# q in units of 512 tokens of two heads from the second batch, the last 64 tokens of all heads as one unit, k and v loaded by pairs of heads

## The chip, the cores and the metric

One core of one Trainium2 chip runs one program. The metric is the device time of an execution in microseconds (us); of several runs the median is given.

## The reference

Two layers, one behind the other. The first is a linear attention with feature maps, for 8 batches of 8 heads, 576 tokens and 64 dimensions; the second a feed-forward network (FFN) with an exact GELU on the 4608 tokens of 512 numbers that the heads give side by side.

```python
def phi(x):                                   # w_phi: 64 x 128
    proj = np.einsum('bhsd,df->bhsf', x, w_phi)
    proj = proj - np.max(np.abs(proj), axis=-1, keepdims=True)
    return np.concatenate([np.exp(proj), np.exp(-proj)], axis=-1)
q_p, k_p = (phi(q), phi(k))
kv = np.einsum('bhsf,bhsd->bhfd', k_p, v)
z = np.sum(k_p, axis=2)
num = np.einsum('bhsf,bhfd->bhsd', q_p, kv)
den = np.einsum('bhsf,bhf->bhs', q_p, z)[..., None] + 1e-06
x = (num / den).transpose(0, 2, 1, 3).reshape(4608, 512)
h = x @ w_in                                  # 512 x 2048
out = (0.5 * h * (1.0 + erf(h / sqrt(2)))) @ w_out   # 2048 x 512
```

## The kernel before

**How the order is made.** The program isn't written in the order in which it runs. Every operation is put into a plan (class `Plan`) with its engine, an estimated cost, a rank, the buffers it reads and writes, and the number of places that each buffer has. `order()` (L109) plays the engines through: at each step the engine that can start first takes its operation with the lowest rank. On TensorE (PE) attention products have a rank lower by `PULL`, but are held back while FFN products run until they sum up to `LUMP` us or one of them has waited for `LINGER` us (L183), so that they come in lumps between FFN products. `emit()` (L245) writes the operations in the order of their planned starts. On the chip each engine, and SP, which issues nearly all DMAs, goes through its own list in that order and waits where an operand isn't there yet. The constants at L790 to L824 are the planner's.

**Attention**, batch after batch (`attention`, L560). `k_rest` and two times `k_quad` (L452) make the sums over k: a quad is two pairs of heads. Per quad one load brings k into kt (524 KB), one v into vt (665 KB); each has two places. Per pair, `k_unit` projects k on PE (pk, eight products of 128 columns), DVE takes the maximum of the magnitudes (mx) and subtracts it, ACT takes both exponentials (ek), PE sums them with v (kv, 40 products of 65 columns, the last of which gives z), and ACT copies that to kvn. The last 64 tokens of k of all heads go through one smaller unit first (pk_r, er).

`q_pair` (L484) then takes the 576 tokens of a pair of heads in two halves of 288 (`HS`): a load (qt), the projection of both heads on PE (pq, the "q unit", two products), a copy by ACT into pc, the maximum over partitions by GpSimd (POOL: `partition_all_reduce`, mb), a subtraction on DVE, two exponentials on ACT (ef). In batches 0 and 1 (`ND`) the product with kvn gives numerator and denominator together (the "d unit", 65 rows). From batch 2 on the numerators are a product of their own ("n unit", pn), and the denominators go another way: DVE weighs the features with z (un), POOL sums them over partitions (db), and row 0 is stored to d_d. xo carries the numerators to x_d in DRAM. `quotients` (L549) loads the denominators of one half of a batch (dc), takes the reciprocal and stores it to r_d.

**FFN.** 18 blocks of 256 tokens. `tokens` (L581) loads a block's numerators (xr, from x_d) and reciprocals (into xh, from r_d), and DVE multiplies and splits the product into a high and a low part (xh, xl). In blocks 0 to 7 (`block`, L623) `up` makes twelve products of 256 columns into ph for each 128 hidden units, ACT takes the GELU twice, DVE the low part (gl), and PE the down-projection into po. The 32 pieces of w_in and w_out are loaded and split by DVE and ACT at the start (`split_weight`), into places named w_i and w_o. Blocks 8 to 17 (`seven`, L695) need a down-projection of seven block products in place of eight; for it sums of w_out's quarters are made (planned from 177.8 us on) and stored to t_d, and `fetch_sums` (L682) loads them into tw0 to tw7. These places lie where attention's lay, so their loads wait for the last operation that uses a place of `EARLIER` (L300).

Places that the change touches: `EARLIER = dict(kr=1, kt=2, vt=2, mx=2, er=2, ek=2, kvn=4, un=1, db=1, qt=2, pc=2, mb=1, ef=2, xo=2, dc=2)`. Products of attention are in plain fp32, and each leaves two records in the trace (an n unit eight, a k projection sixteen); FFN's are in a shorter type and leave one. All matrix products go through the helper at L330, so rows name them by their tiles; likewise the subtractions and additions of L371 and the copies of L365.

Of the kernel before, what the change touches and what calls it, by code (L numbers as in the profile page):

```python
# [59 lines left out]
class Plan:  # L60
# [227 lines left out]
def fused_kernel(ctx: ExitStack, tc: tile.TileContext, qT, kT, va, w_st, w_in, w_out, out):  # L288
# [131 lines left out]

    def k_unit(b, nm, kt, at, cs, e, early, k):
# [26 lines left out]

    def k_quad(b, g, kvs, rank, rest):  # L452
# [9 lines left out]
        for p in range(2):  # L462
            e = [sb[EARLY_EK[p] if b == 0 else "ek"]([P, 2, 4, NF], F32, f"ek_{nm}_{p}_{s}") for s in (1, 0)][::-1]
            k_unit(b, f"{nm}_{p}", kt, lambda c: kt()[:, c * P : (c + 1) * P], range(4 * p, 4 * p + 4), e, EARLY_PK[p] if b == 0 else "pp", k)
            acc = ps["kv"]([P, 4, D + 1], F32, f"kv_{nm}_{p}")
# [15 lines left out]
            kvs[2 * g + p] = kvn  # L481


    def q_pair(b, p, kvs, rank, halves=(0, 1)):  # L484
# [4 lines left out]
        for half in halves:  # L489
            nm = f"{b}_{p}_{half}"  # L490
            ss = slice(half * HS, half * HS + HS)
            qt = sb["qt"]([P, HS], F32, f"qt_{nm}")
# [4 lines left out]
            op("pe", PAIR_Q, lambda pq=pq, qt=qt: [
                mm(pq()[:, j, :HS], lhsT=wst()[64 * j : 64 * j + 64], rhs=qt()[64 * j : 64 * j + 64], start=True, stop=True) for j in range(2)
            ], r=[qt, wst], w=[pq], also=[pc], kind="q", **k(1))
            copy("act", act(2 * HS, True), pc, lambda pq=pq: pq()[:, :, :HS], [pq], [pc], **k(1))  # L500
            op("pool", 2.28, lambda mb=mb, pc=pc: nc.gpsimd.partition_all_reduce(  # L501
                mb(), pc(), P, bass_isa.ReduceOp.absmax), r=[pc], w=[mb], port="max", **k(1))
            tt("dve", dve(2 * HS), pc, pc, mb, ALU.subtract, [pc, mb], [pc], **k(1))
# [362 lines left out]
```

## Time and profile before

| | before |
|---|---|
| median of 3 runs | 1075.69 us (1075.23 to 1076.4) |
| profiled execution | 1074.26 us, span 1072.5 us |
| granted clock of PE, mean | 0.986 |
| PE busy | 1040.8 us (97%) |
| weight loads on PE (beside the products) | 910.0 us (85%) |
| DVE busy | 737.5 us (69%) |
| ACT busy | 617.5 us (58%) |
| POOL busy | 328.2 us (31%) |
| DMA | 107.11 MB, mean 100 GB/s |

The span goes from the first to the last instruction of the profiled execution; its own time is 1.8 us longer. Busy times count instructions in work, whichever engine they wait for otherwise. PE is the engine to follow: a share of 97% says that little of the span passes without a product, but not which of the products' time is columns and which is the step from one kind of product to another; that takes pieces of the chain of waits from single stretches. A granted clock of 1.00 is the higher of PE's two levels (2.4 GHz).

### The profile page before, as it was taken

How to read it: one execution, taken by the hardware profiler on the slowest of the kernel's cores; microseconds unless marked ns; L12 is line 12 of the kernel's file. 1: busy time of each engine (PE TensorE's matmuls, PEld its weight loads, DVE VectorE, ACT ScalarE, POOL GpSimd, SP SyncE). 2: the span in 40 equal slices, each digit the busy share in tenths (PEclk: the TensorE clock that was granted, in tenths of full speed). 3: DMA queues.
4: the chain of work that ended last, by engine and by line, in shares of the span. 5: the costliest groups of instructions: out<-in, count | busy, mean ns of one | idle time of the engine just before them, and what ended most of it. 6: DMA issues, size and time to landing. Idle time of an engine off the chain costs nothing.

```text
span 1072.5 us, 24197 instructions
## 1 busy us (share of the span) xinstructions
PE 1040.8 (97%) x9855; PEld 910.0 (85%) x9855; DVE 737.5 (69%) x1327; ACT 617.5 (58%) x1067; POOL 328.2 (31%) x116
## 2 busy tenths in 40 slices
PE   7979989999999999999999999999999999999997
PEld 4647857887887888787788889999999999999997
DVE  4989999979988999757657532566466465565454
ACT  4867878676866776677676633344344344343343
POOL 2231033645566665866766520000000000000000
PEclk7988999999999999999999999999999999999999
DMA  7676564335344434322122158021021021021000
GB/s 266 214 205 194 176 192 123 102 113 166 103 134 141 134 110 143 94 80 83 46 59 71 37 182 296 21 61 41 20 60 41 21 60 40 20 61 40 2 21 20
DMA packets 87393, 107.11 MB, mean 100 GB/s; under 512 B 25121, under 2 KB 68289, under 8 KB 87281
## 3 DMA queue, kind: packets, MB, share of 16 engines
q1 hardware_dynamic: 87136, 105.30, 32.3%
q8 instruction: 77, 1.26, 0.5%
q14 instruction: 36, 0.29, 0.1%
q10 hardware_dynamic: 144, 0.26, 0.1%
HBM read 75.87 MB, written 29.66 MB: 98 GB/s over the span
## 4 chain that ended last, share of the span: by engine, by line
PE 78%; DVE 11%; ACT 5%; issue 3%; DMA 2%; POOL 0%; SPq 0%; ACTq 0%; POOLq 0%; DVEq 0%
PE ph L330 33%; PE po L330 13%; PE pa L330 10%; PE pb L330 8%; PE pn L330 5%; PE kv L330 4%; PE pq L330 3%; PE pk L330 2%; DVE pc L371 1%; ACT ek L440 1%; DVE ts L371 1%; DVE mx L435 1%; DMA xh<-r_d 1%; DVE ek L371 1%; ACT L632 1%
## 5 line engine op out<-in xcount | busy, mean ns | idle before, releaser
L330 PE MATMUL ph<-xh,w_i 128*128 128x256 f32 x2304 | 413.3, 277 | 0.0
L330 PEld LDWEIGHTS ph<-xh,w_i 128*128 128x128 f32 x2304 | 355.9, 188 | 4.7 <-issue 4.2
L330 PE MATMUL ph<-xl,w_i 128*128 128x256 f32 x1152 | 318.6, 277 | 0.0
L536 POOL PARTITION_ALL_REDUCE db<-un x48 | 183.9, 3831 | 128.6 <-DVE un L533 123.1
L330 PEld LDWEIGHTS ph<-xl,w_i 128*128 128x128 f32 x1152 | 216.3, 188 | 0.4
L501 POOL PARTITION_ALL_REDUCE mb<-pc x64 | 147.1, 2299 | 169.9 <-ACT pc L365 116.0
L371 DVE TENSOR_TENSOR sg<-ga 128x256 f32<-128x256 f32 (+1 forms) x240 | 84.7, 376 | 149.7 <-ACT ga L709 149.0
L330 PE MATMUL po<-w_o,gh 128*128 128x512 f32 (+1 forms) x519 | 164.8, 399 | 2.4 <-DVE w_o L371 1.9
L709 ACT ACTIVATE ga<-ph 128x512 f32<-128x512 f32 x80 | 48.0, 600 | 158.3 <-PE ph L330 156.6
L330 PEld LDWEIGHTS po<-w_o,gh 128*128 128x128 f32 x519 | 93.3, 188 | 30.7 <-issue 4.7
L330 PE MATMUL pa<-w_o,oh 128*128 128x256 f32 x640 | 112.8, 276 | 0.0
L330 PE MATMUL pn<-ef,kvn 128*64 128x288 f32 (+1 forms) x512 | 97.4, 423 | 8.9 <-ACT xo L365 8.9
L507 ACT ACTIVATE ef<-pc 128x576 f32<-128x576 f32 x128 | 82.2, 678 | 39.5 <-DVE pc L371 31.4
L330 PE MATMUL po<-w_o,gl 128*128 128x512 f32 (+1 forms) x288 | 101.0, 369 | 0.3 <-DVE gl L371 0.3
L330 PEld LDWEIGHTS pa<-w_o,oh 128*128 128x128 f32 x640 | 96.2, 188 | 0.0
L371 DVE TENSOR_TENSOR gl<-ph,gh 128x512 fp32r<-128x512 f32 x64 | 43.9, 687 | 64.7 <-ACT ph L633 60.6
L330 PE MATMUL pa<-w_o,ol 128*128 128x256 f32 x320 | 88.3, 276 | 0.0
L371 DVE TENSOR_TENSOR pc<-pc,mb 128x576 f32<-128x576 f32 x64 | 77.7, 1215 | 14.4 <-POOL mb L501 14.3
L440 ACT ACTIVATE ek<-ek 128x1024 f32<-128x1024 f32 x64 | 67.9, 1061 | 31.4 <-DVE ek L371 30.6
L330 PE MATMUL pb<-tw,uh 128*128 128x256 f32 x480 | 85.6, 276 | 0.0
L330 PEld LDWEIGHTS pn<-ef,kvn 128*64 128x64 f32 (+1 forms) x512 | 39.7, 138 | 41.3 <-ACT xo L365 15.8
L330 PEld LDWEIGHTS pb<-tw,uh 128*128 128x128 f32 x480 | 72.2, 188 | 0.0
(71 smaller groups left out, 1610.4 us busy)
## 6 DMA issues: line engine op xcount, KB each, us to landing
vt<-in_va_dram SPq DMA_DIRECT2D x16, 650.0 KB
t_d<-ts SPq DMA_DIRECT2D x40, 256.0 KB
qt<-in_qT_dram SPq DMA_DIRECT2D x64, 144.0 KB
out_dram<-ob SPq DMA_DIRECT2D x35, 256.0 KB
kt<-in_kT_dram SPq DMA_DIRECT2D x16, 512.0 KB
raw_i<-in_w_in_dram SPq DMA_DIRECT2D x16, 512.0 KB
raw_o<-in_w_out_dram SPq DMA_DIRECT2D x16, 512.0 KB
x_d<-xo SPq DMA_DIRECT2D x48, 144.0 KB
```

Of the source, the lines that this page charges most:

```text
L330: return tc.keep_in_program_order(nc.tensor.matmul(*a, **kw))
L371: op(eng, cost, lambda: e.tensor_tensor(out=dst(), in0=a(), in1=b(), op=o), r=r, w=w, **kw)
L435: op("dve", dve(256 * n, True), lambda: nc.vector.tensor_reduce(out=mx(), in_=xs(), axis=AX.X, op=ALU.max, apply_absolute_value=True), r=[ ...
L440: op("act", act(256 * n), lambda s=s: nc.scalar.activation(e[s](), e[1](), AF.Exp, scale=1.0 - 2.0 * s), r=[e[1]], w=[e[s]], table="exp", ...
L501: op("pool", 2.28, lambda mb=mb, pc=pc: nc.gpsimd.partition_all_reduce(mb(), pc(), P, bass_isa.ReduceOp.absmax), r=[pc], w=[mb], port="max ...
L507: op("act", act(2 * HS), lambda ef=ef, pc=pc, s=s: nc.scalar.activation(ef()[:, s], pc(), AF.Exp, scale=1.0 - 2.0 * s), r=[pc], w=[ef], ta ...
L536: op("pool", 3.8, lambda db=db, un=un: nc.gpsimd.partition_all_reduce(db(), un(), P, bass_isa.ReduceOp.add), r=[un], w=[db], port="add", * ...
L632: op("act", act(2 * TB, True) + 0.016, lambda gh=gh, ph=ph: nc.scalar.activation(gh(), ph(), AF.Gelu), r=[ph], w=[gh], table="gelu", rank= ...
L709: op("act", act(2 * TB, True) + 0.037, lambda ph=ph, ga=ga: nc.scalar.activation(ga(), ph(), AF.Gelu), r=[ph_all], w=[ga], table="gelu", a ...
```

## The change

From batch 1 on the 576 tokens of a pair of heads are cut into 512 and 64 where they were cut into 288 and 288 (`PIECES`); batch 0 stays at 288. The first 512 tokens go through `q_pair` as one unit of twice 512 columns. The last 64 tokens of all four pairs go through a new function, `q_rest`, as one unit of twice 256 columns: one projection, one maximum, one subtraction and two exponentials for all eight heads; the numerators (16 small products, since each head has its own kvn for either sign) fill one PSUM tile, and are stored to x_rest, which `tokens` loads with one DMA. `q_front` and `q_sum` hold what both have in common. The sum of the weighed features is written over pc, so un has no places of its own any more. The two exponentials have a tile each (ef, three places). kvn has seven places in place of four, and zb keeps z of all pairs for the rest unit. The quotients of the 512 tokens are taken before the rest unit, those of the 64 behind it.

k and v are loaded by pairs of heads: kt 262 KB, vt 333 KB, eight loads a batch for four. From batch 1 on kt and vt have one place each, of a pair's size; batch 0's eight loads have places of their own, those of w_o8 to w_o15, which are free until these weights come. The projection of k waits for the rest unit's projection two batches before (`behind`), an order among PE's own instructions. The planner's costs are extended by the new POOL shapes, and fourteen of its constants have new values; two of them stand below.

```diff
+HM = 512
+HR = S - HM
+PIECES = [((0, HS), (HS, HS))] + [((0, HM), (HM, HR))] * (B - 1)
...
-    EARLIER = dict(kr=1, kt=2, vt=2, mx=2, er=2, ek=2, kvn=4, un=1, db=1, qt=2, pc=2, mb=1, ef=2, xo=2, dc=2)
+    EARLIER = dict(kr=1, kt=1, vt=1, mx=2, er=2, ek=2, kvn=7, zb=2, db=1, qt=2, pc=2, mb=1, ef=3, xo=2, dc=2)
...
-        op("pe", n * PAIR_K, proj, r=[kt, wst], w=[x], also=[mx], kind="k", **k())
+        op("pe", n * PAIR_K, proj, r=[kt, wst], w=[x], also=[mx], kind="k", behind=last_pq.get(b - 2, ()), **k())
...
+    early = lambda i: plan.pool(spool, f"w_o{8 + i}", 1)
...
-        kt = sb["kt"]([P, 8 * P], F32, f"kt_{nm}")
-        op("sp", 0.06, lambda: nc.sync.dma_start(out=kt(), in_=kT[b, g, :, : 8 * P]), w=[kt], kb=524, **k())
-        vt = sb["vt"]([P, 20, D + 1], F32, f"vt_{nm}")
-        op("sp", 0.06, lambda: nc.sync.dma_start(out=vt(), in_=va[b, g]), w=[vt], kb=665, **k())
+        kts, vts = [], []
         for p in range(2):
+            kt = (early(4 * g + p) if b == 0 else sb["kt"])([P, 4 * P], F32, f"kt_{nm}_{p}")
+            op("sp", 0.06, lambda kt=kt, p=p: nc.sync.dma_start(out=kt(), in_=kT[b, g, :, 4 * P * p : 4 * P * (p + 1)]), w=[kt], kb=262, **k())
+            vt = (early(4 * g + 2 + p) if b == 0 else sb["vt"])([P, 10, D + 1], F32, f"vt_{nm}_{p}")
+            op("sp", 0.06, lambda vt=vt, p=p: nc.sync.dma_start(out=vt(), in_=va[b, g, :, p]), w=[vt], kb=333, **k())
...
+            if b >= ND:
+                if "z" not in kvs:
+                    kvs["z"] = sb["zb"]([P, 4, 4], F32, f"zb_{b}")
+                z = kvs["z"]
+                op("act", act(4) + 0.05, lambda z=z, kvn=kvn, p=p: nc.scalar.copy(out=z()[:, 2 * g + p], in_=kvn()[:, :, D]), r=[kvn], w=[z], **k())
...
+    def q_front(nm, n, load, kb, k, main):
+        qt = sb["qt"]([P, n], F32, f"qt_{nm}")
+        op("sp", 0.06, lambda: load(qt), w=[qt], kb=kb, **k(1))
+        pc = sb["pc"]([P, 2, n], F32, f"pc_{nm}")
+        mb = sb["mb"]([P, 2, n], F32, f"mb_{nm}")
+        pq = ps["pp"]([P, 2, 512], F32, f"pq_{nm}")
+        pq_op = op("pe", n * 4 / 2400 + 0.014, lambda: [
+            mm(pq()[:, j, :n], lhsT=wst()[64 * j : 64 * j + 64], rhs=qt()[64 * j : 64 * j + 64], start=True, stop=True) for j in range(2)
+        ], r=[qt, wst], w=[pq], also=[pc], kind="q", **k(1))
+        copy("act", act(2 * n, True), pc, lambda: pq()[:, :, :n], [pq], [pc], **k(1))
+        most = f"max{main}"
+        op("pool", plan.SPENT[most], lambda: nc.gpsimd.partition_all_reduce(
+            mb(), pc(), P, bass_isa.ReduceOp.absmax), r=[pc], w=[mb], port=most, **k(1))
+        tt("dve", dve(2 * n), pc, pc, mb, ALU.subtract, [pc, mb], [pc], **k(1))
+        ef = [sb["ef"]([P, 2, n], F32, f"ef_{nm}_{s}") for s in range(2)]
+        for s in range(2):
+            op("act", act(2 * n), lambda s=s: nc.scalar.activation(ef[s](), pc(), AF.Exp, scale=1.0 - 2.0 * s), r=[pc], w=[ef[s]], table="exp", **k())
+        return pc, ef, pq_op
+
+    def q_sum(nm, n, pc, k, main):
+        db = sb["db"]([P, 2, n], F32, f"db_{nm}")
+        total = f"add{main}"
+        op("pool", plan.SPENT[total], lambda: nc.gpsimd.partition_all_reduce(db(), pc()[:, :2], P, bass_isa.ReduceOp.add), r=[pc], w=[db], port=total, **k())
+        return db
...
-            ss = slice(half * HS, half * HS + HS)
-            qt = sb["qt"]([P, HS], F32, f"qt_{nm}")
...
-            mb = sb["mb"]([P, 2, HS], F32, f"mb_{nm}")
...
-            op("pe", PAIR_Q, lambda pq=pq, qt=qt: [
...
-            ef = sb["ef"]([P, 2, 2, HS], F32, f"ef_{nm}")
+            at, n = PIECES[b][half]
+            main = "" if n == HS else " main"
+            pc, ef, _ = q_front(nm, n, lambda qt, at=at, n=n: nc.sync.dma_start(out=qt(), in_=qT[b, p, :, at : at + n]), n * 0.512, k, main)
...
-            un = sb["un"]([P, 2, HS], F32, f"un_{nm}")
-            db = sb["db"]([P, 2, HS], F32, f"db_{nm}")
...
+            one = lambda s, j, kvn=kvn: kvn()[:, 2 * s + j, D : D + 1]
+            for j in range(2):
+                op("dve", dve(n, fast=True) + 0.06, lambda pc=pc, ef=ef, one=one, j=j: nc.vector.tensor_scalar(
+                    out=pc()[:, j], in0=ef[0]()[:, j], scalar1=one(0, j), scalar2=None, op0=ALU.mult), r=[ef[0], kvn], w=[pc], **k())
+            for j in range(2):
+                op("dve", dve(n) + 0.06, lambda pc=pc, ef=ef, one=one, j=j: nc.vector.scalar_tensor_tensor(
+                    out=pc()[:, j], in0=ef[1]()[:, j], scalar=one(1, j), in1=pc()[:, j], op0=ALU.mult, op1=ALU.add),
+                   r=[ef[1], kvn, pc], w=[pc], **k())
+            db = q_sum(nm, n, pc, k, main)
...
+            pn = ps["pn"]([P, n], F32, f"pn_{nm}")
+            op("pe", n * 8 / 2400 + 0.012, lambda pn=pn, kvn=kvn, ef=ef: [
+                mm(pn()[64 * j : 64 * j + 64], lhsT=kvn()[:, 2 * s + j, :D], rhs=ef[s]()[:, j], start=s == 0, stop=s == 1)
                 for s in range(2) for j in range(2)
...
+    def q_rest(b, kvs, rank):
+        k = lambda x=0: dict(rank=next(rank))
+        plan.stream = "q"
+        nm, n = f"{b}_rest", 4 * HR
+        pc, ef, pq_op = q_front(nm, n, lambda qt: nc.sync.dma_start(
+            out=qt().rearrange("r (p t) -> r p t", p=4), in_=qT[b, :, :, HM:].rearrange("p r t -> r p t")), 131, k, " rest")
+        last_pq[b] = [pq_op]
+        kv = [kvs[p] for p in range(4)]
+        of = lambda s, j, p: ef[s]()[:, j, p * HR : (p + 1) * HR]
...
+        if b < ND:
+            for j in range(2):
+                pn = ps["pn"]([P, n], F32, f"pn_{nm}_{j}")
+                op("pe", 8 * mm4_cost(D + 1, HR), lambda pn=pn, j=j: [
+                    mm(pn()[: D + 1, p * HR : (p + 1) * HR], lhsT=kv[p]()[:, 2 * s + j, :], rhs=of(s, j, p), start=p == 0 and s == 0, stop=p == 3 and s == 1,
+                       skip_group_check=True) for p in range(4) for s in range(2)], r=[*kv, *ef], w=[pn], kind="d", **k())
...
+            return
+        z = kvs["z"]
+        un = sb["pc"]([P, 4, n], F32, f"un_{nm}")
+        for s in range(2):
+            tt("dve", dve(2 * n), lambda s=s: un()[:, 2 * s : 2 * s + 2].rearrange("r j (p t) -> r j p t", p=4),
+               lambda s=s: ef[s]().rearrange("r j (p t) -> r j p t", p=4),
+               lambda s=s: z()[:, :, 2 * s : 2 * s + 2].rearrange("r p j -> r j p").unsqueeze(3).to_broadcast([P, 2, 4, HR]), ALU.mult, [ef[s], z], [un], **k())
+        tt("dve", dve(2 * n), lambda: un()[:, :2], lambda: un()[:, :2], lambda: un()[:, 2:], ALU.add, [un], [un], **k())
+        db = q_sum(nm, n, un, k, " rest")
+        for j in range(2):
+            op("sp", 0.06, lambda j=j: nc.sync.dma_start(out=heads(j), in_=db()[:1, j].rearrange("o (p t) -> o p t", p=4)), r=[db], w=[d_d[b][1]], kb=1, **k())
+        pn = ps["pn"]([P, n], F32, f"pn_{nm}")
+        op("pe", 8 * PAIR_V, lambda: [
+            mm(pn()[64 * j : 64 * j + 64, p * HR : (p + 1) * HR], lhsT=kv[p]()[:, 2 * s + j, :D], rhs=of(s, j, p), start=p == 0 and s == 0, stop=p == 3 and s == 1,
+               skip_group_check=True) for p in range(4) for s in range(2) for j in range(2)], r=[*kv, *ef], w=[pn], kind="n", **k())
...
-                q_pair(b, p, kvs, rank)
-        for half in range(2):
-            quotients(b, half, rank)
+                q_pair(b, p, kvs, rank, (0,))
+        quotients(b, 0, rank)
+        q_rest(b, kvs, rank)
+        quotients(b, 1, rank)
...
+            kw = dict(w=[xr], rank=rank(0) - 8)
+            if b and h:
+                op("sp", 0.06, lambda b=b, s=s, n=n, o=o: nc.sync.dma_start(out=xr()[:, :, o : o + n], in_=x_rest[b]()[:, :, s : s + n]),
+                   r=[x_rest[b]], kb=n * 2.048, **kw)
...
-LUMP = 5.47
-LINGER = 4.41
+LUMP = 5.52
+LINGER = 3.07
```

In the built program, PE's list around the numerators of batch 5's first pair, before (ph: up-projection of block 4; pn: numerators; pq: projection of q; the number behind a name only tells tiles apart):

```order
L330 MATMUL ph_4_2_5125<-xl_4_3975,w_i3_1_1073 128x256
L330 MATMUL ph_4_2_5125<-xh_4_3786,w_i3_1_1073 128x256
L330 MATMUL pn_5_0_0_5166<-ef_5_0_0_5079,kvn_5_0_0_4467 64x288 x4
L330 MATMUL pq_5_1_0_5175<-qt_5_1_0_4908,wst_114 128x288 x2
L330 MATMUL ph_4_3_5180<-xh_4_3786,w_i0_1_862 128x256
L330 MATMUL ph_4_3_5180<-xl_4_3975,w_i0_1_862 128x256
```

and after (po: down-projection of block 4; kv: sums over k of batch 6):

```order
L334 MATMUL po_4_4862<-w_o3_786,gh_4_1_4860 128x512 x2
L334 MATMUL po_4_4862<-w_o3_786,gl_4_1_4874 128x512
L334 MATMUL pn_5_0_0_4914<-ef_5_0_0_0_4871,kvn_5_0_0_4137 64x512 x2
L334 MATMUL pn_5_0_0_4914<-ef_5_0_0_1_4893,kvn_5_0_0_4137 64x512 x2
L334 MATMUL kv_6_0_0_4924<-vt_6_0_0_4669,er_6_0_4717 64x65 x2
L334 MATMUL kv_6_0_0_4924<-vt_6_0_0_4669,er_6_1_4709 64x65 x2
```

The n unit of 288 columns with the q unit of the next pair behind it has become one n unit of 512 columns, and a kv unit of batch 6 stands behind it.

SP's list at the start of the program, behind the load of w_phi, before (kr, kt and vt: k and v of batch 0; raw: the first piece of w_in):

```order
L447 DMA kr_0_120<-in_kT_dram 128x2x128
L459 DMA kt_0_0_122<-in_kT_dram 128x1024
L461 DMA vt_0_0_124<-in_va_dram 128x1300
L459 DMA kt_0_1_126<-in_kT_dram 128x1024
L461 DMA vt_0_1_128<-in_va_dram 128x1300
L383 DMA raw_i0_0_131<-in_w_in_dram 128x512
```

and after:

```order
L451 DMA kr_0_120<-in_kT_dram 128x2x128
L467 DMA kt_0_0_0_122<-in_kT_dram 128x512
L469 DMA vt_0_0_0_124<-in_va_dram 128x650
L467 DMA kt_0_0_1_126<-in_kT_dram 128x512
L469 DMA vt_0_0_1_128<-in_va_dram 128x650
L467 DMA kt_0_1_0_131<-in_kT_dram 128x512
L469 DMA vt_0_1_0_133<-in_va_dram 128x650
L467 DMA kt_0_1_1_135<-in_kT_dram 128x512
L469 DMA vt_0_1_1_137<-in_va_dram 128x650
L387 DMA raw_i0_0_139<-in_w_in_dram 128x512
```

The four loads of kt and vt have become eight of half the size, and the first piece of w_in is issued behind them as before.

SP's list from the last store of denominators to the first loads of tw, before:

```order
L537 DMA d_d7_1_7006<-db_7_3_1_7461 1x576
L692 DMA w_o4_1172<-t_d4_3851 128x2x256
L692 DMA w_o5_1190<-t_d5_4170 128x2x256
L555 DMA dc_7_1_7518<-d_d7_1_7006 128x18
L558 DMA r_d7_1_7550<-dc_7_1_7518 128x18
L690 DMA tw_0_7593<-t_d0_2384 128x1536
L690 DMA tw_1_7595<-t_d1_2672 128x1536
```

and after (xh_9: reciprocals for block 9):

```order
L603 DMA d_d7_1_7211<-db_7_rest_7160 4x1x64
L762 DMA w_o11_1736<-t_d3_3302 128x2x256
L762 DMA w_o12_1981<-t_d4_3628 128x2x256
L619 DMA dc_7_1_7238<-d_d7_1_7211 128x4
L762 DMA w_o13_2018<-t_d5_4152 128x2x256
L622 DMA r_d7_1_7268<-dc_7_1_7238 128x4
L670 DMA xh_9_7285<-r_d4_0_4660 64x4x256
L761 DMA tw_0_7321<-t_d0_2283 128x1536
L761 DMA tw_1_7323<-t_d1_2634 128x1536
```

The last store of denominators is that of the rest unit now, in two parts (one is shown), the load of dc_7_1 has 4 columns where it had 18, and a load of reciprocals for block 9 stands ahead of the first tw.

## Rows read from the trace of the kernel before

**Rows 1.** The page: busy time and share of PE over the span with its instructions, then the slices of the span (PE, DVE, and the clock that PE was granted).
```profile
PE 1040.8 (97%) x9855; PEld 910.0 (85%) x9855; DVE 737.5 (69%) x1327; ACT 617.5 (58%) x1067; POOL 328.2 (31%) x116
...
PE   7979989999999999999999999999999999999997
...
DVE  4989999979988999757657532566466465565454
...
PEclk7988999999999999999999999999999999999999
```

**Rows 2.** Busy time of each engine in four stretches: stretch, its length, then PE, PEld, DVE, ACT, POOL busy us (instructions), PE's granted clock, DMA share, GB/s.
```profile
0.00:90.00 90.00, 71.95 (x909) 47.91 (x910) 69.68 (x97) 60.25 (x102) 26.31 (x15) 0.85 0.72 226
90.00:200.00 110.00, 105.26 (x975) 82.15 (x975) 105.17 (x162) 86.25 (x140) 31.80 (x12) 1.00 0.52 158
200.00:625.00 425.00, 421.80 (x4169) 342.10 (x4166) 330.28 (x473) 298.53 (x453) 268.10 (x90) 1.00 0.35 103
625.00:1073.00 448.00, 441.78 (x3814) 437.85 (x3810) 232.34 (x598) 172.50 (x375) 2.02 (x1) 1.00 0.19 57
```

**Rows 3.** The chain of waits, pieces in order of time: start us, us, what. Two pieces of an early stretch, a quiet stretch of block 4 and batches 4 to 6, and one piece of block 7 and 8 (a piece lasts to the next start).
```profile
38.89 1.11 PE pn L330 x4
40.01 0.65 PE pk_r L330 x8
...
409.81 0.69 PE pq L330 x4
410.50 1.58 PE ph L330 x12
...
421.59 1.12 PE pn L330 x8
...
434.37 2.48 PE kv L330 x80
436.85 1.09 PE pk L330 x16
...
631.23 5.44 PE ph L330 x48
```

**Rows 4.** Groups of instructions by line and shape: the two POOL groups for 200 to 625 us, the PE weight load for the whole span. Columns: line, engine, operation, tiles, shape, count | busy us, mean ns of one | idle before, by releaser.
```profile
L536 POOL PARTITION_ALL_REDUCE db<-un x46 | 176.7, 3841 | 118.7 <-DVE un L533 113.2 <-DMA d_d<-db 2.5 <-issue 2.4
...
L501 POOL PARTITION_ALL_REDUCE mb<-pc x44 | 99.0, 2249 | 41.6 <-ACT pc L365 25.6 <-DVE pc L371 6.6 <-DVE un L533 6.2
...
L330 PEld LDWEIGHTS pn<-ef,kvn 128*65 128x65 f32 x128 | 16.4, 144 | 23.3 <-ACT xo L365 12.5 <-issue 2.2 <-ACT ek L440 0.8
```

**Rows 5.** Instructions of the first 16 us in order of time, all engines: start us, us, engine, line, operation, tiles, count [idle before, releaser]. SPq rows issue DMAs.
```profile
2.59 0.47 SPq L459 DMA_DIRECT2D kt<-in_kT_dram  x1
...
10.51 0.71 PE L330 MATMUL pk_r<-wst,kr 64*128 64x128 f32 x8 [0.74 <-ACT pc L365]
...
11.88 0.75 DVE L371 TENSOR_TENSOR pc<-pc,mb 128x576 f32<-128x576 f32 x1
...
13.33 3.78 PE L330 MATMUL pk<-wst,kt 64*128 64x128 f32 x32 [2.11 <-issue]
...
15.45 1.23 DVE L435 TENSOR_REDUCE mx<-pk 128x8 f32<-128x1024 f32 x1 [2.21 <-PE pk L330]
```

**Rows 6.** From the end of attention to block 8: first three pieces of the chain of waits (start us, us, what), then SP's DMA issues in order of time (start us, us, what).
```profile
624.40 1.12 PE pn L330 x8
...
653.11 5.44 PE ph L330 x48
...
665.54 1.06 PE pb L330 x9
...
629.41 0.32 SPq L537 DMA_DIRECT2D d_d<-db  x1
...
632.21 0.33 SPq L555 DMA_DIRECT2D dc<-d_d  x1
635.10 0.33 SPq L558 DMA_DIRECT2D r_d<-dc  x1
636.85 4.04 SPq L690 DMA_DIRECT2D tw<-t_d  x8
641.27 2.25 SPq L692 DMA_DIRECT2D w_o<-t_d  x2
...
656.58 0.58 SPq L599 DMA_DIRECT2D xh<-r_d  x1
```

**Rows 7.** One sum on POOL and the DVE instruction that starts behind it, in order of time (start us, us, what).
```profile
479.16 3.67 POOL L536 PARTITION_ALL_REDUCE db<-un  x1
...
479.29 3.09 DVE L371 TENSOR_TENSOR pc<-pc,mb 128x576 f32<-128x576 f32 x1 [2.28 <-POOL mb L501]
```

**Rows 8.** Who SP's queue waited for, over the span: waiting line, releaser, us in total, times, longest us.
```profile
SPq L459 <- PE pk L330: 22.8, 8, 6.6
```

More of the change, by code (lines that the diff above doesn't have):

```diff
@@ L69 @@
     SHAPE = {"f": 0, "k": 1, "q": 1, "v": 2, "n": 2, "w": 3, "d": 4}
-    READS = {"max": 1.12, "add": 2.38, "sum": 1.27}
+    READS = {"max": 1.12, "add": 2.38, "max main": 1.99, "add main": 4.23, "max rest": 1.0, "add rest": 2.12}
+    SPENT = {"max": 2.28, "add": 3.8, "max main": 3.75, "add main": 6.45, "max rest": 2.07, "add rest": 3.42}
     WINDOW = 3.413
@@ L79, in pool, with op @@
         return lambda shape, dt, name: Buf(self, tag, lambda: (pool() if callable(pool) else pool).tile(shape, dt, tag=tag, name=name, bufs=bufs))
-    def op(self, eng, cost, fn, r=(), w=(), also=(), rank=0.0, table=None, late=0.0, kb=0, duty=1.0, kind="f", port=None, part=None, after=()):
+    def op(self, eng, cost, fn, r=(), w=(), also=(), rank=0.0, table=None, late=0.0, kb=0, duty=1.0, kind="f", port=None, part=None, after=(), behind=()):
         o = Op()
@@ L86, in op @@
         o.reopen = bool(after)
-        deps = set(after)
+        deps = {*after, *behind}
         for b in r:
@@ L414, in weights @@
         plan.since = 0.0
-    d_d, r_d = ([[Buf(plan, None, lambda b=b, h=h, nm=nm: dpool.tile([H, HS], F32, name=f"{nm}{b}_{h}")) for h in range(2)] for b in range(B)]
-                for nm in ("d_d", "r_d"))
-    x_d = [[[Buf(plan, None, lambda b=b, p=p, h=h: dpool.tile([P, HS], F32, name=f"x_d{b}_{p}_{h}")) for h in range(2)]
+    d_d, r_d = ([[Buf(plan, None, lambda b=b, h=h, n=n, nm=nm: dpool.tile([H, n], F32, name=f"{nm}{b}_{h}")) for h, (_, n) in enumerate(PIECES[b])]
+                 for b in range(B)] for nm in ("d_d", "r_d"))
+    x_d = [[[Buf(plan, None, lambda b=b, p=p, h=h, n=n: dpool.tile([P, n], F32, name=f"x_d{b}_{p}_{h}")) for h, (_, n) in enumerate(PIECES[b])]
             for p in range(4)] for b in range(B)]
+    x_rest = [Buf(plan, None, lambda b=b: dpool.tile([P, 4, HR], F32, name=f"x_rest{b}")) for b in range(B)]
+    last_pq = {}
     def k_unit(b, nm, kt, at, cs, e, early, k):
@@ L490, in q_pair @@
             nm = f"{b}_{p}_{half}"
-            ss = slice(half * HS, half * HS + HS)
-            qt = sb["qt"]([P, HS], F32, f"qt_{nm}")
-            op("sp", 0.06, lambda qt=qt, ss=ss: nc.sync.dma_start(out=qt(), in_=qT[b, p, :, ss]), w=[qt], kb=147, **k(1))
-            pc = sb["pc"]([P, 2, HS], F32, f"pc_{nm}")
-            mb = sb["mb"]([P, 2, HS], F32, f"mb_{nm}")
-            pq = ps["pp"]([P, 2, 512], F32, f"pq_{nm}")
-            op("pe", PAIR_Q, lambda pq=pq, qt=qt: [
[L498 to L503, printed above, removed]
-            ef = sb["ef"]([P, 2, 2, HS], F32, f"ef_{nm}")
+            at, n = PIECES[b][half]
+            main = "" if n == HS else " main"
+            pc, ef, _ = q_front(nm, n, lambda qt, at=at, n=n: nc.sync.dma_start(out=qt(), in_=qT[b, p, :, at : at + n]), n * 0.512, k, main)
             kvn = kvs[p]
-            for s in range(2):
-                op("act", act(2 * HS), lambda ef=ef, pc=pc, s=s: nc.scalar.activation(ef()[:, s], pc(), AF.Exp, scale=1.0 - 2.0 * s),
-                   r=[pc], w=[ef], table="exp", **k())
             x_to, d_to = x_d[b][p][half], d_d[b][half]
@@ L807 @@
 ND = 2
-LUMP = 5.47
-LINGER = 4.41
+LUMP = 5.52
+LINGER = 3.07
 PAIR_K = 0.224
-PAIR_Q = 0.494
-PAIR_N = 0.972
 PAIR_V = 0.118
@@ L835, in _layout @@
     v6 = v.reshape(B, 2, 2, 2, S, D)
-    va = np.ones((B, 2, P, 20, D + 1), v.dtype)
-    va[:, :, :, 16:] = 0
+    va = np.ones((B, 2, P, 2, 10, D + 1), v.dtype)
+    va[..., 8:, :] = 0
     for p in range(2):
         full = v6[:, :, p, :, :512].reshape(B, 2, 2, 4, P, D).transpose(0, 1, 4, 3, 2, 5).reshape(B, 2, P, 8, D)
-        va[:, :, :, 8 * p : 8 * p + 8, :D] = full
-        rows = va[:, :, 64 * p : 64 * p + 64, 16 + 2 * p : 18 + 2 * p]
+        va[:, :, :, p, :8, :D] = full
+        rows = va[:, :, 64 * p : 64 * p + 64, p, 8:]
         rows[..., :D] = v6[:, :, p, :, 512:].transpose(0, 1, 3, 2, 4)
```

96 lines of the change are left out of this document (49 added, 47 removed).

## Prediction

> **What bounds the kernel now.** I read the busy shares and slices first [rows 1]: TensorE (PE) is busy 97% of the span of 1072.5 us, no other compute engine over 69%. A share over the whole span hides where it is lost, so next I cut the span at the points where the work changes [rows 2]. From 0 to 90 us the feed-forward (FFN) part can't start: PE is idle 18 of 90 us and its granted clock averages 0.85; DVE, which splits the weights and feeds the feature maps, is busy 70 of 90. From 90 to 200 us PE idles 4.7 us. From 200 to 625 us, the rest of the attention, it idles 3.2 of 425 us, at clock 1.00. Behind 625 us only FFN is left, with nothing that the change edits. So from 90 to 625 us time comes off only if PE itself has less to do or waits less.
>
> PE's work there isn't all columns. In the chain of waits of a quiet stretch [rows 3] sixteen records of the k projection take 1.09 us and eight of the same shape (pk_r) 0.65: eight records of 128 columns cost 0.44 us, 0.43 ns a column, and 0.21 us is left over that no column explains. A q unit (four records of 288 columns, 0.50 us by that price) takes 0.69: 0.19 fixed. An n unit (numerator product, eight records, 0.99) takes 1.12: 0.13 fixed. A d unit (numerator with denominator row, one record at a time, so twice the price: 0.99) takes 1.11: 0.12 fixed. Twelve FFN records take 1.58 right behind such a unit, against 5.44 for 48 inside a run, 1.36 for twelve: 0.22 fixed. These fixed parts stand wherever PE goes from one kind of product to another.
>
> **The change, part by part.** *Fewer, longer q units.* Columns are the same before and after (each batch has 576 tokens of 8 heads either way), so only the fixed parts change. I counted in the two built programs the groups of like work on PE from the first FFN product on: q 53 before, 32 now; n 48 and 30; d 14 and 9; k and v unchanged at 29 and 24; FFN 60 and 67, because the retuned table cuts FFN more finely. That is 21 x 0.19 + 18 x 0.13 + 5 x 0.12 = 6.9 us less and 7 x 0.22 = 1.5 us more: **5.4 us less**. It lies on the path, since PE waits for next to nothing there [rows 2]. Ahead of the first FFN product the count of groups is 42 in both.
>
> *The rest unit* (64 tokens of all heads) is new. Its n product has 32 records of 64 columns with a weight load for each; the nearest row is the kv unit, 80 records of 65 columns in 2.48 us [rows 3], 0.031 us each, so 0.99 us against 0.88 by columns, six times. Its d product (batch 1 alone, two groups of 16 records) costs 0.9 by columns, and up to 16 x 0.144 = 2.3 us if each weight load shows [rows 4]. Together +0.2 to +3.5 us; I take +0.5, since the kv row is the nearer one: there loads of this size hide nearly whole.
>
> *DVE, ACT, POOL.* POOL's maxima and sums over partitions take 2.25 and 3.84 us for 576 columns [rows 4], 49 us a batch. Scaled by columns the new ones take 4.0 and 6.8, the rest 2.0 and 3.4, again 49 us a batch; POOL is busy for 268 of these 425 us now [rows 2]. DVE and ACT drop some fixed costs, and ACT gains four table loads of 1.28 us. I cost all of this at nothing, under PE's queued FFN work; what it costs without that cover is the first rival.
>
> *Loads.* In batch 0 each k and v load is cut in two, and all eight have places of their own (the buffers of w_o8 to w_o15). PE waits 2.11 us for the first k tile, from its r unit to 13.33 us, though the load was issued at 2.59; DVE waits 2.21 us for it in turn [rows 5]. With half as many bytes in that load the wait shrinks by 0 to 2.1 us. DVE, nearly full until FFN starts, passes part of it on; I take **-1.0 us**. From batch 1 on there is one k and one v buffer of a pair's size where there were two of two pairs; that is the second rival.
>
> *Hand-over to block 8.* Its weight sums (tw) may be loaded when all attention buffers are free. Before, the last attention product starts at 624.40 us, the denominators come back by way of dc and r_d, tw is issued at 636.85, and the load that waits for the first tw is issued at 641.27, 16.9 us behind that product; tw is first read at 665.54 [rows 6]. In the new order only 17.2 us of columns and about 1 us of fixed parts stand between the last attention product and that first read, where it was 41.1 us. So it fits, with about 1 us to spare. A load of xh_9 also stands ahead of tw on SP now; it waits for the end of block 7's last up-projection, as before (issued 656.58, behind the first half of the piece that starts at 653.11). From there the columns to the first read of tw are 8.2 us; two issues and a landing of 4.4 take some 5.8. I take 0, with up to +6 if POOL's last sum comes one long sum (6.8 us) late.
>
> Sum: -5.4 + 0.5 - 1.0 = **-5.9 us**. Against the profiled execution (1074.26 us, span 1072.5) that gives 1068.4; against the median of the runs shown (1075.69), 1.4 us above the profiled one, it gives **1069.8 us**.
>
> **Rivals.** *A, slower: POOL's longer hold of DVE reaches PE.* A DVE subtraction that begins at 479.29, just behind a POOL sum of 3.67 us (479.16), takes 3.09 us; a free one takes 0.75, so it stood still until about 481.6, two thirds of the sum [rows 5, 7]. At 1024 columns the sum is 6.5 us and the hold 4.4 instead of 2.5. DVE works in order; behind a held instruction stand gl (which PE's down-projection needs), the k maximum and the next weight sum. Today little of this reaches PE: 3.2 us of idle over 90 POOL instructions [rows 2]. An FFN half-group of 2.7 us (half of the 5.44) covers a hold of 2.5, but not one of 4.4. If half of the 24 long sums catch a gl so, and PE waits the 1.9 us that are new, that is +23 us: about **1093**. It decides from 5.9/24 = 0.25 us a sum. Against it: POOL stands still for over a third of the stretch, and a second FFN half-group often stands between.
> The Trainium skill, "SBUF — State Buffer", section "Who interferes with whom", says that of a GpSimd instruction and a DVE instruction with two SBUF inputs the first to start holds the shared port for the whole instruction. Here the trace disagrees in length: DVE went on 1.2 us before the sum ended.
> As a mechanism of this kernel, a hold to the end of the new sum would last 6.5 us where the row shows 2.5 now, 4.0 us more for each of the 12 caught sums, 48 us in all: about **1118**. Since the row shows DVE going on early, I give it 0.01.
>
> *B, no change: one k and one v buffer.* A pair's v load is issued only when the previous pair's kv unit is done, its k load behind the k projection. Its landing lies between the 2.8 us from one small transfer to the next that needs it (629.41 to 632.21) and the 4.4 us of tw [rows 6], and up to 10.7 us in the crowded start [rows 5]. In batch 1 the new order has three close places, by columns and fixed parts: 2.9 us of PE work between the second and third k projection, 4.1 and 5.5 between kv units; later batches have 6.5 us or more everywhere. At those three PE can wait from 0 to 7.8, 6.6 and 5.2 us. At 2 us each the gain is gone: **1076**. For it: SP already waits 22.8 us for PE to free k tiles [rows 8]. Against it: DVE and ACT, not loads, set that stretch.
>
> *C, no change: the hand-over.* The hand-over's upper end of +6 us gives **1076** as well.
>
> *D, more.* The start gives the full 2.1 us, and the 7.9 us that PE idles from 90 to 625 us [rows 2] halve with fewer hand-offs: 1069.8 - 1.1 - 4.0 = **1064.7**.
>
> **How the numbers follow.** Forecast (1066 to 1073) 0.62; D 0.10; B 0.09, C 0.06; A 0.12, with the whole-instruction hold 0.01 above it. The two orders leave no doubt that the units are merged. A difference of 0.2% (2.15 us) is about what a measurement of this kernel can tell from none. Faster: forecast and D, with a little of B and C, 0.74. Same: the rest of B and C, 0.13. Slower: A and the whole-instruction hold, 0.13. The range for 8 in 10 reaches from the deeper part of D, 1063, to behind B and C, 1078; it leaves out A, its whole-instruction form and the edges of D. The unknown prices (+0.2 to +3.5, 0 to -2.1, 0 to +6) lie inside it.
>
> **What would show it.** Right: 21 q groups and 18 n groups fewer on PE, each new q unit about 1.07 us and each n unit 1.9; PE idle from 90 us to the end of attention below 10 us; the first FFN product within 3 us of where it stood; tw issued before PE needs it. Wrong: PE gaps ended by gl behind a DVE instruction that a sum of 6 us holds (A); gaps ended by a v load in batch 1 (B); a gap ahead of block 8's pb (C); or a longer stretch before FFN starts, which the sum takes as nearly unchanged.

## The result and the profile after

The changed kernel takes 1086.57 us (median of 4 runs, 1085.34 to 1087.84) beside 1075.46 us of the kernel before: a ratio of 1.0099 (95% interval 1.0086 to 1.0112), 11.1 us slower, where 5.9 us faster were forecast. The profiled execution took 1086.7 us, its span is 1084.9.

Busy time in four stretches of the changed kernel, columns as in [rows 2] (PE, PEld, DVE, ACT, POOL, then clock, DMA share, GB/s):

```profile
0.00:90.00 90.00, 71.90 (x916) 47.37 (x917) 72.08 (x100) 61.36 (x103) 27.10 (x14) 0.91 0.72 220
90.00:200.00 110.00, 94.68 (x829) 71.54 (x828) 101.35 (x145) 78.34 (x116) 31.21 (x7) 0.94 0.47 140
200.00:625.00 425.00, 417.46 (x4115) 335.16 (x4114) 283.43 (x373) 289.56 (x403) 226.20 (x51) 0.99 0.35 105
625.00:1085.00 460.00, 454.12 (x3909) 445.95 (x3907) 240.62 (x611) 187.23 (x391) 20.92 (x5) 1.00 0.19 59
```

From 90 to 200 us PE is idle for 15.3 us where it was 4.7, and its clock averages 0.94 where it was 1.00. To see what pays for what, I cut each step from the start of one PE product to the next into its columns (0.44 ns an FFN column, 0.42 a column of attention, twice that in a d unit), PE's idle time, and a rest, which stands either where the kind of product changes or inside a run of FFN products:

| us | before | after | difference |
|---|---|---|---|
| up to the first FFN product | 90.5 | 89.5 | -1.1 |
| from there to block 8: columns | 506.2 | 504.3 | -1.9 |
| rest where kinds change | 42.2 | 35.0 | -7.2 |
| rest inside FFN runs | 8.8 | 16.5 | +7.6 |
| PE idle | 7.9 | 22.9 | +14.9 |
| from block 8 on | 416.8 | 416.9 | 0.0 |

The columns of the whole program are the same before and after; the 1.9 us of them that are missing here are attention's, and now stand ahead of the first FFN product. So the fixed parts came down somewhat more than forecast, and idle time with slower FFN products ate three times as much. Who PE waited for in the changed kernel (us in total, times, longest us):

```profile
PE po L334 <- DVE gl L375: 7.1, 4, 4.4
...
PE ph L334 <- DVE w_i L375: 5.1, 1, 5.1
PE po L334 <- DVE w_o L375: 5.0, 1, 5.0
```

Three single waits, at 163.8, 183.1 and 346.8 us, make 14.5 us. The first, in order of time (start us, us, engine, line, operation, tiles):

```profile
161.17 7.76 POOL L522 PARTITION_ALL_REDUCE db<-pc  x1 [10.73 <-DVE pc L556]
...
162.88 4.76 DVE L553 TENSOR_SCALAR pc<-ef,kvn 128x512 f32<-128x512 f32 x1
...
163.55 0.28 PE L334 MATMUL ph<-xl,w_i 128*128 128x256 f32 x1
...
168.16 0.68 DVE L375 TENSOR_TENSOR w_i<-wt_i,w_i 128x512 fp32r<-128x512 f32 x1
...
168.89 0.79 PE L334 MATMUL ph<-xh,w_i 128*128 128x256 f32 x2 [5.06 <-DVE w_i L375]
```

A sum on POOL begins at 161.17. A DVE instruction that takes 0.48 us elsewhere begins under it and takes 4.76: a stop, as I call it. Behind it in DVE's list stands the last step of a weight piece, and PE's next product needs that piece. The second sum stops two steps of a later piece in the same way (4.56 and 1.54 us for 0.42 each), and PE waits from 183.1 us:

```profile
180.24 6.20 POOL L522 PARTITION_ALL_REDUCE db<-pc  x1 [11.31 <-DMA d_d<-db]
...
180.59 4.56 DVE L391 TENSOR_SCALAR wt_o<-wt_o 128x512 f32<-128x512 f32 x1
...
185.18 1.54 DVE L393 TENSOR_SCALAR wt_o<-wt_o 128x512 uint32<-128x512 uint32 x1
...
187.37 0.68 DVE L375 TENSOR_TENSOR w_o<-wt_o,w_o 128x512 fp32r<-128x512 f32 x1
...
188.10 0.79 PE L334 MATMUL po<-w_o,gh 128*128 128x512 f32 x1 [5.04 <-DVE w_o L375]
```

The third stop is of the tokens of a block, xr, with gl behind it. DVE had already waited 1.51 us there for a load of reciprocals:

```profile
344.05 7.02 POOL L522 PARTITION_ALL_REDUCE db<-pc  x1 [3.09 <-DVE pc L556]
...
346.60 3.97 DVE L375 TENSOR_TENSOR xr<-xr,xh 128x1024 f32<-128x1024 f32 x1 [1.51 <-DMA xh<-r_d]
...
350.49 0.68 DVE L375 TENSOR_TENSOR gl<-ph,gh 128x512 fp32r<-128x512 f32 x1
...
351.22 0.79 PE L334 MATMUL po<-w_o,gl 128*128 128x512 f32 x1 [4.38 <-DVE gl L375]
```

Each of the three is paid for a second time. Five-microsecond stretches around the first and the third:

```profile
160.00:165.00 5.00, 1.86 (x13) 1.42 (x11) 5.00 (x8) 1.77 (x3) 3.83 (x1) 1.00 0.56 206
165.00:170.00 5.00, 1.11 (x5) 1.11 (x6) 5.00 (x5) 1.13 (x2) 3.93 (x1) 0.56 0.00 0
170.00:175.00 5.00, 5.00 (x34) 4.88 (x33) 5.00 (x10) 2.16 (x4) 0.00 (x0) 0.76 0.00 0
...
350.00:355.00 5.00, 3.78 (x9) 3.00 (x10) 4.96 (x7) 1.39 (x2) 1.07 (x1) 0.50 0.00 0
355.00:360.00 5.00, 5.00 (x37) 4.90 (x36) 3.21 (x6) 3.19 (x4) 0.00 (x0) 0.83 0.42 132
```

Behind some 5 us without a product PE goes on at the lower of its two levels (0.50 and 0.56 are close to 1.2 of 2.4 GHz), and products take about twice as long for a few microseconds: 2.4 to 2.7 us more each time, which is nearly all of the 7.6 us in the table.

Why the first two stops had no counterpart before shows in the trace of the kernel before, where the last weight piece is done just ahead of the first sum:

```profile
176.24 0.68 DVE L371 TENSOR_TENSOR w_o<-wt_o,w_o 128x512 fp32r<-128x512 f32 x1
...
178.77 3.59 POOL L536 PARTITION_ALL_REDUCE db<-un  x1 [6.69 <-DVE un L533]
```

In the changed kernel two sums come ahead of the last piece, which is done at 190.08 us, 13 us later.

### The profile page after: what moved, and what is told of

Same layout as the page of the kernel before. It is cut to its first block, busy times and chain, and to the rows that moved or that the text cites. A ratio compares the mean times of both kernels' runs of the same rounds, so it can differ in the third digit from the quotient of the medians.

```text
span 1084.9 us, 23613 instructions
## 1 busy us (share of the span) xinstructions
PE 1038.2 (96%) x9763; PEld 900.0 (83%) x9763; DVE 697.5 (64%) x1228; ACT 616.5 (57%) x1008; POOL 305.4 (28%) x77
## 4 chain that ended last, share of the span: by engine, by line
PE 80%; DVE 8%; DMA 4%; ACT 3%; issue 3%; POOL 1%; SPq 0%; DVEq 0%; ACTq 0%; POOLq 0%
PE ph L334 33%; PE po L334 14%; PE pa L334 10%; PE pb L334 7%; PE kv L334 5%; PE pn L334 4%; PE pk L334 2%; PE pq L334 2%; DMA xh<-r_d 1%; DMA x_d<-xo 1%; DVE pc L375 1%; DVE pc L553 1%; DVE ts L375 1%; PE pn_rest L334 1%; POOL mb L511 1%
## 5 line engine op out<-in xcount | busy, mean ns | idle before, releaser
L334 PE MATMUL ph<-xh,w_i 128*128 128x256 f32 x2304 | 419.8, 279 | 7.0 <-DVE w_i L375 5.1
L522 POOL PARTITION_ALL_REDUCE db<-pc x24 | 151.0, 6290 | 137.2 <-DVE pc L556 112.7
L511 POOL PARTITION_ALL_REDUCE mb<-pc x36 | 121.2, 3368 | 161.9 <-ACT pc L369 128.2
L334 PE MATMUL pn<-ef,kvn 128*64 128x512 f32 (+2 forms) x288 | 80.5, 561 | 5.6 <-ACT xo L369 5.6
L516 ACT ACTIVATE ef<-pc 128x1024 f32<-128x1024 f32 (+1 forms) x72 | 68.1, 972 | 17.5 <-DVE pc L375 17.2
L334 PEld LDWEIGHTS po<-w_o,gl 128*128 128x128 f32 x281 | 53.9, 192 | 21.3 <-DVE gl L375 9.6
L703 ACT ACTIVATE gh<-ph 128x512 fp32r<-128x512 f32 x64 | 38.2, 597 | 54.2 <-PE ph L334 52.1
```

The costliest lines, as they stand in the source:

```text
L334: return tc.keep_in_program_order(nc.tensor.matmul(*a, **kw))
L511: op("pool", plan.SPENT[most], lambda: nc.gpsimd.partition_all_reduce(mb(), pc(), P, bass_isa.ReduceOp.absmax), r=[pc], w=[mb], port=most, ...
L516: op("act", act(2 * n), lambda s=s: nc.scalar.activation(ef[s](), pc(), AF.Exp, scale=1.0 - 2.0 * s), r=[pc], w=[ef[s]], table="exp", **k())
L522: op("pool", plan.SPENT[total], lambda: nc.gpsimd.partition_all_reduce(db(), pc()[:, :2], P, bass_isa.ReduceOp.add), r=[pc], w=[db], port= ...
L703: op("act", act(2 * TB, True) + 0.016, lambda gh=gh, ph=ph: nc.scalar.activation(gh(), ph(), AF.Gelu), r=[ph], w=[gh], table="gelu", rank= ...
```

## The experiments

**Theory 1 (hold):** sums on POOL stop DVE, and stopped instructions reach PE; in its first form each of the 24 long sums costs a part, because it is long. **Theory 2:** the new table is late with the weights whatever POOL does. **Theory 3:** the new constants make a slow order by themselves. **Theory 4 (place)** was formed behind the first four runs: a few sums cost nearly everything, by what is queued on DVE behind the instruction that they stop.

**Short sums.** The same order, but each long sum covers 64 columns a head in place of 512 (its store is two DMAs that repeat them).

```diff
+        cut = slice(0, 64) if n == HM else slice(0, n)
-        ... partition_all_reduce(db(), pc()[:, :2], P, bass_isa.ReduceOp.add)
+        ... partition_all_reduce(db()[:, :, cut], pc()[:, :2, cut], P, bass_isa.ReduceOp.add)
```

> The changed kernel in its own order, but each of the 24 POOL sums of twice 512 columns covers only twice 64 of them (the stored denominators repeat these 64, so the output is not the reference's); its store is two DMAs. Theory 1 (hold): the long sums stop DVE, and three such stops reach PE at 164, 183 and 347 us, 14.5 us of idle and about 7.5 us of products at the lower clock. Without them the time is 22 us less, 1063 to 1067 us, and the three gaps are gone. Theory 2 (the new table asks for the weights too early or too late): DVE is behind with the weights whatever POOL does; the gaps at 164 and 183 stay at least by half, and the time stays at 1074 us or above.

Measured: 1069.04 us, ratio to the kernel before 0.9939 (0.9922 to 0.9956). 17.5 us come back, and idle from the first FFN product to block 8 falls from 22.9 to 8.6 us; the run missed its 1067 by 2 us. Theory 2 falls as the main cause. A part of it stays: PE still waits 1.9 and 1.1 us for pieces of w_i at 163.4 and 165.9 us, which the kernel before doesn't do, and from 165 to 170 us its granted clock is 0.68, although neither gap is near 5 us. The time is close to the forecast's 1069.8, in part by luck: the fixed parts save more than forecast, and these waits and slower products give some of it back.

**Split sums.** Two calls of 512 columns in the place of one; then the maxima likewise.

```diff
+        calls = [slice(0, 2)] if n < HM else [slice(j, j + 1) for j in range(2)]
+        ... [partition_all_reduce(db()[:, c], pc()[:, c], P, bass_isa.ReduceOp.add) for c in calls]
```

> The changed kernel in its own order, but each sum of twice 512 columns is two calls of 512 columns, one behind the other, in the place of the one; everything is computed. Theory 1 (hold): DVE gets in between the calls, a stop lasts 2.2 us in place of 4.4, and each of the three gaps shrinks by half at least, so that the clock falls less: 1070 to 1080 us. Theory 2 (weights out of step): no change, 1084 to 1088 us.

> As the run with split sums, and the maxima of twice 512 columns are two calls too. Theory 1 (hold): stops of up to 2.0 us under a maximum halve as well; since few of them reach PE, it is 0 to 3 us faster than with split sums alone. Theory 2: 1084 to 1088 us.

Measured: 1086.05 us (1.0097; 1.0082 to 1.0112) and 1086.14 (1.0092; 1.0077 to 1.0107): no change. The split kernel at the first place:

```profile
159.96 7.92 POOL L523 PARTITION_ALL_REDUCE db<-pc  x2 [8.41 <-DVE pc L558]
...
161.45 2.73 DVE L558 SCALAR_TENSOR_TENSOR pc<-ef,kvn,pc 128x512 f32<-128x512 f32 x1
164.10 0.68 DVE L395 SCALAR_TENSOR_TENSOR wt_i<-raw_i,wt_i 128x512 uint32<-128x512 uint32 x1
164.70 2.46 DVE L391 TENSOR_SCALAR wt_o<-wt_o 128x512 f32<-128x512 f32 x1
...
168.47 0.58 PE L334 MATMUL ph<-xh,w_i 128*128 128x256 f32 x1 [6.00 <-ACT w_i L369]
```

Either call stops one DVE instruction for 2.0 us, with one step between them, and PE waits 6.0 us for a piece of w_i that ACT can make only when DVE, late by both stops, is done with wt_i at 167.76. Both times are what theory 2 expected, but the short sums had spoken against it. What the two runs show is that the length of one call doesn't decide, which is against theory 1 in its first form: in DVE's way were the same 1024 columns at the same place.

**The new constants alone**, in the kernel before.

> The kernel before with the fourteen planner constants of the changed one, nothing else. Theory 3 (the new constants make an order that is late by itself): 1081 us or more. Theories 1 and 2, where the long sums or their neighbours are needed for the loss: within 4 us of 1075.5.

Measured: 1081.11 us, 1.0052 (1.0037 to 1.0067). By its number this is theory 3's case, if barely: the table isn't neutral, and 14 constants move the old kernel by 5 us. But there is no wait for weights in it; its loss is spread over the first FFN product (1.4 us later), rests between kinds (+2.5), idle (+1.6) and slower products inside FFN runs (+3.0). One of its gaps is like the third stop, under a sum of 576 columns; it reaches PE as a wait of 1.39 us, by way of ACT, whose copy of ob stands behind a step that waits for DVE:

```profile
326.60 4.05 POOL L536 PARTITION_ALL_REDUCE db<-un  x1
...
327.11 3.55 DVE L371 TENSOR_TENSOR xr<-xr,xh 128x1024 f32<-128x1024 f32 x1
```

**Single sums.** As short sums, but for chosen ones (`nm in ("2_0_0", "2_1_0")`, then with `"4_0_0"`, then all but these three).

> The changed kernel in its own order; only the first two sums on POOL (batch 2, first and second pair) cover twice 64 columns in place of twice 512 (the denominators of these tokens are wrong by that). Theory 4 (place): these two come ahead of the last pieces of the weights, at 161 and 180 us, while DVE finishes the last piece at 190; before, the first sum started at 179, behind the last piece at 177. They alone make the gaps at 164 and 183, 10.1 us of idle and about 5 us at the lower clock: 1070 to 1074 us, last piece at 183 us or earlier, the gap at 347 stays. Theory 1 in its first form (every long sum costs a little): 2 of 24 sums are worth 2 of 24 parts of the 17.5 us, so 1084 to 1086 us.

> The changed kernel in its own order; three sums cover twice 64 columns in place of twice 512 (the denominators of these tokens are wrong by that): the first two of batch 2, and the first of batch 4, under which DVE's multiplication of xr stood still at 347 us. Place theory: these three carry the whole loss, 1068 to 1071 us, as with all 24 short. Theory 1 in its first form (each of the 24 costs a part): 1074 us or more.

> The reverse: those three stay long, the other 21 cover twice 64 columns. Place theory: the three gaps stay, 1084 to 1088 us. Theory 1 in its first form: 1072 to 1076 us.

| short sums | us | ratio to before (95%) | less than the changed kernel |
|---|---|---|---|
| first two of batch 2 | 1076.47 | 1.0004 (0.9993 to 1.0016) | 10.1 |
| these and the third | 1071.86 | 0.9964 (0.9952 to 0.9976) | 14.7 |
| the other 21 | 1083.63 | 1.0072 (1.0055 to 1.0089) | 2.9 |
| all 24 | 1069.04 | 0.9939 (0.9922 to 0.9956) | 17.5 |

The kernel before, measured anew beside each run of this section, gave 1074.7 to 1075.9 us. The parts add up (14.7 + 2.9 = 17.6), and theory 1 in its first form falls. The place theory's own ranges were each missed by a little: two sums by 2.5 us (1074 was its bound), three by 0.9 (1071), the other 21 by 0.4 (1084). Three sums carry 84% of the loss, not all of it. The trace of the changed kernel agrees: four other sums stop DVE just as long (4.1 to 4.4 us, at 266.2, 279.4, 435.4 and 465.9 us), and only behind the first of them does PE wait for gl, for 0.71 us. 4_0_0 gives 4.6 of the 7 us that its gap and clock cost: with it short, PE still waits 2.8 us there for gl, since xr stands 2.63 us for the reciprocals' load anyway.

**Later sums.** A rule in the plan, the sums of batch 2 not before 176 us of planned time; and the same with the constants searched anew.

```diff
+        since, plan.since = plan.since, 176 if nm[:2] == "2_" else plan.since
         op("pool", plan.SPENT[total], ...)
+        plan.since = since
```

> The changed kernel with one more rule in the plan: the sums of batch 2 may not start before 176 us of planned time, behind the last piece of the weights (171 us planned); all is computed, and the order behind that moves. Theory 4 (place): the gaps at 164 and 183 go, 1069 to 1076 us, with the last piece below 182 us. Theory 1 in its first form: long sums only stop something else, 1082 us or more.

> As the run with late sums, with the fifteen constants searched anew by planned time under the condition that no sum starts ahead of the last piece of the weights. Place theory: the 7 us of fixed parts that the longer units save show in the time, 1065 to 1072 us. Theory 1 in its first form: 1082 us or more.

Measured: 1076.40 us (1.0013; 1.0002 to 1.0024) and 1077.81 (1.0014; 1.0002 to 1.0025). The first number is 0.4 us above its range, and what came back didn't come by the mechanism: planned times only sort the lists, and POOL, with nothing ahead of the sum in its own, started it at 162.54 us all the same. Its 5.06 us gap stayed; the other two went with the new order. The second missed its 1072 by 6 us: the first sum ran at 157.3 us, with the last piece done at 191.48. A rule on POOL was the wrong handle.

**The loads alone**, in the kernel before: eight loads a batch, one place each, constants searched anew.

> The kernel before with k and v loaded by pairs (the eight loads of batch 0 in places of their own, one place each for kt and vt behind that), units of 288 tokens as before; the planner's constants are searched anew for it by planned time, since the old ones leave attention's end too late. Place and hold theories: the loads are worth 0 to 2 us, 1073 to 1079 us with what the new order adds. If the one place for kt and vt were the cause: 1080 us or more, with waits of PE on DMAs of vt or kt.

Measured: 1080.86 us, 1.0047 (1.0032 to 1.0062). The time is one that was expected if the one place for kt and vt were the cause, but PE waits for no load of k or v in it, so that cause is out. Its new table starts FFN 5.7 us later, and what the loads are worth can't be told from this run.

**Later weighing.** The handle that works: DVE's weighing of batch 2's features stands behind the last weight piece in DVE's own list, and the sum needs the weighing. Constants searched anew, two outcomes.

```diff
+            since, plan.since = plan.since, FIRST if b == ND else plan.since
             for j in range(2):
                 op("dve", ...)   # the four weighing steps
...
+            plan.since = since
             db = q_sum(nm, n, pc, k, main)
```

> The changed kernel with one more rule in the plan: DVE may not weigh the features of batch 2 before 169.57 us of planned time, so that these instructions stand behind the last piece of the weights in DVE's list, and the sums that need them behind both; the planner's constants are searched anew by planned time, alone and with its costs a little larger; all is computed. Place theory: on the chip no sum starts ahead of the last piece, no wait of PE for w_i or w_o is longer than 3 us, and the 7 us of fixed parts come out: 1064 to 1072 us. If long sums cost wherever they stand (theory 1 in its first form): 1080 us or more.

> The same rule with another outcome of the search for the constants (planned 3.6 us longer). Place theory: no sum ahead of the last piece, 1066 to 1076 us; what differs from the run beside it is where the later sums happen to stop an instruction that PE needs.

Measured: 1070.99 us, 0.9962 (0.9948 to 0.9976), and 1076.95, 1.0017 (1.0004 to 1.0029). The first lies in its range and beats both kernels, by 3.7 us and about 15; the second missed its 1076 by 1 us. The first one's trace (the profiled run was its slowest, 1075.09 us):

```profile
182.21 0.68 DVE L375 TENSOR_TENSOR w_o<-wt_o,w_o 128x512 fp32r<-128x512 f32 x1
...
188.57 6.28 POOL L522 PARTITION_ALL_REDUCE db<-pc  x1 [27.55 <-DVE pc L557]
```

No weight waits are left, PE idles 10.9 us from the first FFN product to block 8, and rests between kinds are 37.7 us. In the second no sum comes ahead of the last piece either; its FFN starts 9.8 us later than in the first (97.9 us), and a sum stops a step ahead of gl at 268 us (2.6 us of PE). The rule takes the two stops away. The constants differ in both runs as well, so how much of the 15 us is the rule's own they don't tell; the 6 us between them are luck of the order.

## Why the prediction was wrong, point by point

**Failed: "I cost all of this at nothing, under PE's queued FFN work".** What came in its place is 14.5 us of idle in three gaps and some 7.5 us of products at the lower clock. The cover holds for the 21 sums that are worth 2.9 us, all behind 200 us. It doesn't from 90 to 200: there DVE is busy 105.17 of 110 us [rows 2], PE's queued work needs the weight pieces that DVE has yet to finish, and so DVE is the cover itself. I read PE's 4.7 us of idle there as slack; 1.9 us of it were already waits for pieces of w_o, so DVE was barely on time. Behind 200 us the cover failed once, at 346.8 us, where gl stood behind the stopped instruction. The prediction follows PE's and SP's lists; DVE's, around the last weight piece, would have shown the sums' weighing ahead of it.

**Rival A had the mechanism, with the wrong place, count and price.** It put twelve stops of 1.9 us on gl all over the stretch, 23 us. There were three, two of them on weight pieces, of 4.4 to 5.1 us of idle and 2.4 to 2.7 of lower clock, which it had not priced: some 22 us. Its argument from length fell with the split sums: DVE's time lost under sums even shrank from the kernel before to the changed one, from 57.6 us in 32 stops to 43.2 in 18 (each stopped instruction less the shortest of its shape). The prediction's break-even of 0.25 us a sum spreads evenly what hangs on the place.

**Its chance was too low, and the range too narrow.** The reasons against it, that POOL stands still for a third and FFN half-groups cover, were shares of the wrong stretch.

**Right: the fixed parts.** -5.4 and +0.5 us were forecast, -7.2 came: q -4.4, n -3.1, d -0.7, FFN +1.3. A q unit of 512 columns takes 1.06 us and an n unit 1.87, as forecast. The n part was sized a little small, and the rest unit's n product with its 32 weight loads takes 1.08 us, 0.2 above its columns.

**Wrong: the first k load.** The 2.11 us wait is as long as before, with half the bytes:

```profile
12.33 0.68 DVE L375 TENSOR_TENSOR er<-pk_r,mx_r 128x512 f32<-128x512 f32 x1
...
13.11 3.15 PE L334 MATMUL pk<-wst,kt 64*128 64x128 f32 x26 [2.11 <-issue]
```

pk needs the PSUM place that pk_r holds until er has read it, at 13.01 us; before, er ends at 13.24 and pk starts at 13.33. So the wait was not for the load, and the landing of up to 10.7 us that rival B takes from it isn't shown either. FFN's 1.1 us earlier start is not shown as a gain: runs with the same list ahead of it start FFN at 89.5 to 92.7 us.

**Didn't come: B, C, D and the whole-instruction hold.** PE waits 0.5 us in all for a load of v (B). tw is issued at 669.45 us and PE reads it at 676.4 without a wait (C). The idle time that D halves grew threefold. The stop under the sum at 161.17 ends at 167.6, 1.3 us ahead of the sum's end. The Trainium skill, "SBUF — State Buffer", section "Who interferes with whom", has such a hold last the whole instruction; this trace goes on disagreeing.

## What to carry to other kernels

Whether an engine's queued work covers another's stall must be read stretch by stretch, and with it what stands behind the stalled instruction in its list: three of 24 equal sums cost five times as much as the other 21. When a change makes units longer, look which of them now come ahead of the last urgent work of a full engine, and move the work that feeds them in the engine's own list; cutting the long instruction in two didn't help. Each of the three gaps of some 5 us on PE cost half as much again by the lower clock behind it.

## What the runs showed that I had not expected

A sum of 1024 columns takes 6.11 us alone, less than the 6.8 scaled from 576 columns, but 7.8 us where DVE works in its first 1.7 us (161.17 us above). Ten DVE instructions of 256 or 512 columns were stopped by a long sum in its first 3.7 us, and all ten ended 1.3 us ahead of its end, whether they began 0.04 us (435.4) or 3.7 us (228.6) behind its start; two of 1024 columns ended 0.5 us ahead. So how long such a stop lasts hangs on when DVE comes to it. Five more, all of the form TENSOR_SCALAR with 512 columns, began in a sum's last 1.3 us and ended 0.28 us behind it, up to 1.1 us late. Two calls back to back stop DVE twice, for 2.0 us each at the place shown, with room for one DVE step in between.
